# Column-tile projections that share passes with value matmuls, in an attention and MLP kernel on one core

## The chip, the core and the metric

The kernel runs on one core of a Trainium2 chip. The core has a matrix engine (TensorE, PE in the profile), a vector engine (VectorE, DVE), an engine for activation functions (ScalarE, ACT), a general engine (GpSimd, POOL), and SyncE (SP), whose queue issues most of the transfers. The engines run side by side, each with its own instructions in a fixed order, and wait for one another by semaphores. PSUM, the memory that PE writes, has eight banks of 512 fp32 columns here. The metric is the device time of one execution in microseconds (us); less is better.

## The reference

The input is one sequence of 2048 tokens with 512 features. Two blocks read it, and a gate mixes them. `norm` is a layer norm without learned factors, and `shift` moves each quarter of the features by +1, -1, +2 or -2 tokens.

```python
x = A_x                                            # 1 x 2048 x 512
g = sigmoid((x * gate_w).sum(-1))
q, k, v = split(x @ wqkv)                          # 32 heads of 16 features
a = softmax(q @ k.T * 16 ** -0.5) @ v @ wo         # per head, heads side by side
h = gelu(norm(x) @ w1)                             # 512 -> 512
x1 = x + shift(h) @ w2
b = x1 + gelu(norm(x1) @ w3) @ w4                  # 512 -> 1792 -> 512
out = g * a + (1 - g) * b
```

## The kernel before

Attention is most of the work. The queries are taken in four chunks `c` of 512. For each chunk there are 4 groups `G` of 8 heads, and for each group 2 parities `p`: 32 rounds, each of 4 heads at once. A head of a round has 16 key tiles of 128 keys, so a round has 64 score tiles (128 keys by 512 queries) and the kernel 2,048.

A score tile is one matmul with 32 contracted rows (`qk_op`, line 842). Four of them fit beside each other in the array, as row tiles; this mode is called "row". Its exponential is made in one of two ways:

- On ACT (`issue_act`, line 910): two score tiles lie in one PSUM slot of 1024 columns (`psA`, two such slots), and one ACTIVATE (line 922) makes bf16 probabilities of both in a slot of `PA` (8 slots of 1024 columns). Each tile then takes one value matmul. The slot is free again when both have been done.
- On DVE (`issue_dve`, line 932): the tile lies in a `ring` slot of 512 columns (three such slots). DVE turns scores into the bits of a bf16 exponential (line 948). Three shifted copies of a pair of tiles follow, on DVE (line 984) or POOL (line 986), and the sum of four value matmuls smooths the error. So such a tile takes four value matmuls.

A value matmul (`take_pv`, line 1017) contracts 128 keys and writes 17 rows of the accumulator `acc`: the head's sum of probabilities and its 16 features. Each of the four heads of the round has its own column tile of the array, at columns 0, 32, 64 and 96; this mode is called "col". Each column tile has a queue of its own, `pvq[i]`.

Everything else that PE multiplies is a projection: q, k, v, w1 to w4 and the output projection. `gen` (line 525) describes one as a list of units; a unit is four matmuls, one to each column tile (line 532), and all the units add up in one ring slot, which DVE then reads out (`evac`). So scores for DVE and projections share the three ring slots. In this text a pass is a group of up to four matmuls, one to each tile of the array, that run at the same time.

The order of all this is not written by hand. A planner (`Sim`, line 90) plays the engines in the kernel's own build: jobs with a hold time, dependencies, buffers and priorities. `pe_run` (line 190) places matmuls on PE, with a cost `SWITCH` for a change between the row and column modes. What comes out is an order of instructions for each engine, and that order is what the chip runs; no time of the planner's is in it. Whenever the planner's PE is free, `pe_pick` (line 1174) chooses what comes next:

- Score tiles first, if a `psA` slot is free: two for ACT (up to twice), and in the same pass up to `DVE_WAIT` for DVE if a ring slot is free.
- Otherwise column work for at most `MAXU` passes, up to the time at which ACT is expected to give back its slot. `do_gen` takes whole units of the current projection (`cur_gen`, `run_gen` at line 1150): there is one at a time. `do_pv` takes value matmuls, one from each queue that has one ready, for as many passes as keep the filled share over a limit (`PV_FULL`, `PV_IDLE`).
- Otherwise `filler` (line 1258) may put in matmuls with zeros.

`BASE` (line 296) holds the settings of these choices, and `STAGES` (line 321) replaces some of them for each stretch of 32 score tiles (`SEG`). After each round `finish_round` reads `acc` out, and a chain of transfers through SP's queue divides by the sums. At the end of the kernel (lines 1289 to 1344) the last output tiles use the three ring slots and half of a `psA` slot as banks.

Of the kernel before, what the change touches and what calls it, by code (L numbers as in the profile page):

```python
# [47 lines left out]

class Call:
# [28 lines left out]
class Gen:  # L78


    def __init__(self, units, deps, at, name, acq="ring", due=None):
        self.units, self.deps, self.at, self.name = units, deps, at, name
        self.due = due
        self.pos = 0
        self.buf = Buf(acq, 1)
        self.ops = [o for u in units for o in u]
        self.gone = False


class Sim:  # L90
    SWITCH = 95.0
# [64 lines left out]
    def try_engine(self, e):  # L156
        if self.t_free[e] > self.t:
            return False
        best = None
        for j in self.jobs[e]:  # L160
            if j.at > self.tiles:
                continue
            if j.ready is None:
                if any(d.done is None for d in j.deps):
                    continue
                j.ready = self.t
            if any(not self.free[b.cls] for b in j.acq) or j.port and self.lock > self.t:
                continue
            key = (j.prio, j.ready, j.seq)
            if best is None or key < best[0]:  # L170
                best = (key, j)
        if best is None:
            return False
        j = best[1]
        self.jobs[e].remove(j)
        for b in j.acq:
            self.take(b)
        j.start = self.t
        self.emit(self.t, self.in_port_order(e, j.fn) if j.port else j.fn)
        self.t_free[e] = self.t + j.hold  # L180
        if j.port:
            self.lock = self.t + j.hold
        self.busy[e] += j.hold
        self.log.append((e, self.t, j.hold, j.name))
        self.push(self.t + j.hold, None)
        self.pending -= 1
        self.push(self.t + j.hold + j.lat, lambda: self.finish_job(j))
        return True

    def pe_run(self, ops):  # L190
        cur = self.t
        for o in ops:
            if o.mode != self.mode:
                s = max(max(self.arr), cur) + self.SWITCH
                self.mode = o.mode
            elif o.tile is None:
                s = max(max(self.arr), cur)
            else:
                s = max(self.arr[o.tile], cur + self.ISSUE)
# [46 lines left out]
def kernel(  # L246
# [50 lines left out]
        P1_PRIO=0.414,  # L297
        S_PRIO=0.38,
        GP2=0.0,
        GP3=1.0,  # L300
        DVE_STOP=6,
        DVE_STOP_L=8,
        URG=5,
        URG_L=17,
        DVE_ALONE=2,
        EARLY=68,
        SL=(45, 60),
        IDLE_NS=537,
        PD_LOW=0,
# [3 lines left out]
        AHEAD2=9,  # L313
        PV_FULL=0.916,
        PV_IDLE=0.37,
        PRESS=27,
        MAXU=9,
        ROT=0, DUE_SH=0, AT_SH=0,
    )
    SEG = 32  # L320
    STAGES = {0: {'DVE_ALONE': 150, 'EARLY': 2}, 1: {'GP3': 0.6}, 2: {'P1_PRIO': 0.438, 'AT_SH': 120, 'PD_LOW': 2, 'URG_L': 20}, 3: {'DUE_SH': 20, 'URG_L': 19, 'PRESS': 8}, 4: {'GP2': 0.35, 'DVE_WAIT': 4, 'SL': (165, 60), 'URG_L': 14}, 5: {'DVE_STOP_L': 7, 'ROT': 3}, 6: {'ROT': 3, 'URG_L': 20, 'EARLY': 110, 'AT_SH': 120}, 7: {'DVE_STOP': 8}, 8: {'ROT': 2}, 9: {'ROT': 2, 'GP2': 0.2}, 12: {'DVE_STOP_L': 6, 'PA_LOW': 2, 'PV_FULL': 0.686, 'AHEAD2': 10}, 13: {'ROT': 3}, 14: {'GP3': 0.9, 'AT_SH': 120, 'AHEAD2': 10}, 16: {'ROT': 2}, 17: {'URG_L': 16, 'DVE_STOP_L': 6, 'AT_SH': 10, 'PV_IDLE': 0.593}, 18: {'ROT': 2, 'PA_LOW': 3}, 20: {'MAXU': 7, 'AT_SH': 120, 'GP2': 0.35}, 22: {'PV_FULL': 0.805, 'GP2': 0.35}, 23: {'GP2': 0.35}, 25: {'S_PRIO': 0.215, 'DVE_STOP': 7, 'URG': 7}, 26: {'PV_FULL': 0.638, 'DVE_STOP': 8}, 27: {'URG_L': 14, 'PV_IDLE': 0.319, 'DVE_ALONE': 500, 'PD_LOW': 3}, 28: {'DVE_STOP_L': 5, 'PV_FULL': 0.681, 'GP3': 0.8}, 29: {'DVE_WAIT': 4, 'DVE_ALONE': 300, 'URG': 7, 'PV_IDLE': 0.328}, 30: {'PA_LOW': 1, 'URG_L': 19}, 31: {'PA_LOW': 0, 'SL': (165, 180), 'PRESS': 28, 'PD_LOW': 3}, 32: {'DVE_STOP_L': 10, 'P1_PRIO': 0.596, 'ROT': 2, 'S_PRIO': 0.516}, 33: {'PRESS': 54, 'ROT': 3, 'AHEAD2': 7, 'S_PRIO': 0.436}, 34: {'AT_SH': 120, 'P1_PRIO': 0.562, 'AHEAD2': 7}, 35: {'GP3': 0.6}, 36: {'URG': 8, 'AHEAD2': 12}, 37: {'S_PRIO': 0.236, 'AHEAD': 8, 'P1_PRIO': 0.491}, 38: {'P1_PRIO': 0.476, 'ROT': 3}, 39: {'GP3': 0.9, 'AHEAD2': 10, 'URG': 6, 'GP2': 0.1}, 40: {'URG': 3, 'PV_FULL': 0.947, 'DVE_ALONE': 300, 'PD_LOW': 2}, 41: {'DVE_ALONE': 0, 'PV_IDLE': 0.272, 'ROT': 2, 'PD_LOW': 1}, 42: {'DVE_STOP': 7, 'DVE_STOP_L': 10, 'DUE_SH': -8, 'PRESS': 10}, 43: {'URG': 8}, 44: {'GP2': 0.1}, 45: {'URG_L': 18, 'GP2': 0.2}, 46: {'GP3': 0.8}, 47: {'DVE_STOP': 5, 'P1_PRIO': 0.442, 'MAXU': 3, 'PRESS': 11}, 48: {'SL': (5, 20)}, 49: {'SL': (5, 20)}, 50: {'DVE_STOP_L': 5, 'AHEAD2': 8, 'P1_PRIO': 0.218, 'AT_SH': 30}, 51: {'DVE_STOP': 9, 'P1_PRIO': 0.226, 'GP3': 0.6}, 52: {'DVE_WAIT': 5, 'PD_LOW': 3, 'ROT': 2, 'IDLE_NS': 697}, 53: {'ROT': 1}, 54: {'ROT': 1, 'P1_PRIO': 0.201}, 55: {'PA_LOW': 2}, 56: {'EARLY': 60, 'PV_FULL': 0.817, 'P1_PRIO': 0.354}, 57: {'DVE_ALONE': 2, 'PD_LOW': 3}, 58: {'DVE_ALONE': 300, 'GP2': 0.35, 'PRESS': 15}, 59: {'PRESS': 19}, 60: {'DUE_SH': 40, 'PRESS': 20}, 61: {'IDLE_NS': 380}, 62: {'AHEAD': 8, 'GP2': 0.35}, 63: {'ROT': 2}}
# [3 lines left out]
    WIDTHS, RING = (2, 2), 3  # L325

# [9 lines left out]
    def slots(name, n, shape, dt=BF16, where=const):  # L336
# [38 lines left out]
    sim_ring = slots("ring", RING, [P, 512], F32, ps)  # L375
    sim = Sim({
        **{f"psA{w}{n}": slots(f"psA{n}", 1, [P, 512 * w], F32, ps) for n, w in enumerate(WIDTHS)},
        "ring": sim_ring,
        "PA": slots("PA", NPA, [P, 512 * max(WIDTHS)]),
# [145 lines left out]
    def gen(name, at, deps, mms, N=512, due=None):  # L525
# [11 lines left out]
        g = Gen(units, deps, at, name, due=due)  # L537
        gens.append(g)
# [10 lines left out]
    def x_transposes(c, half, dep):  # L549
# [6 lines left out]
        g.ops = [o for u in g.units for o in u]  # L556
        g.buf.users = 2
# [70 lines left out]
    def gate(at):  # L628
# [14 lines left out]
        g2.ops = list(g2.units[0])  # L643
        g2.ops[-1].frees.append(zl)
# [11 lines left out]
        gt.ops = gt.units[0]  # L656
        zb = Buf("ot", 1)
# [252 lines left out]
    def issue_act(got, cls):  # L910
        buf = Buf(cls, 1)
        sim.take(buf)
        ops = []
        for h, (r, (kt, i)) in enumerate(got):
            left[r][i].remove(kt)
            ops.append(qk_op(r, kt, i, lambda h=h: buf.slot[:, h * 512:(h + 1) * 512], buf))
        n = 512 * len(got)
        pb = Buf("PA", len(got))

        hold = 0.833 * n + 67.0  # L920
        exps[:] = [j for j in exps if j.done is None]
        job = act(hold, ops, lambda: nc.scalar.activation(out=pb.slot[:, 0:n], in_=buf.slot[:, 0:n], func=ACT.Exp,  # L922
                                                          scale=0.25), acq=[pb], frees=[buf], prio=3)
        exps.append(job)
        for h, (r, (kt, i)) in enumerate(got):
            c, G, p = rounds[r]
            add_pv(r, i, kt, lambda kt=kt, h_=8 * G + 2 * i + p: V0[:, kt, h_, :],
                   lambda h=h: pb.slot[:, h * 512:(h + 1) * 512], [job, j_v[kt, G // 2]], pb)
            pv_left[r] += 1
# [206 lines left out]
    cur_gen = [None]  # L1136

    def gen_ready():
        if cur_gen[0] is not None:
            return cur_gen[0]  # L1140
# [9 lines left out]
    def run_gen(g, nunits, ops):  # L1150
        if cur_gen[0] is None:
            cur_gen[0] = g
            sim.take(g.buf)
            gens.remove(g)
        took = 0
        while g.pos < len(g.units) and took < nunits:
            ops += g.units[g.pos]
            g.pos += 1
            took += 1
        if g.pos == len(g.units):  # L1160
            cur_gen[0] = None
        return took
# [11 lines left out]
    def pe_pick():  # L1174
# [6 lines left out]
        for _ in range(len(WIDTHS)):  # L1181
# [3 lines left out]
            got = act_tiles(w, used if len(used) + w <= 4 else set())  # L1185
            if not got:
                break
            ops += issue_act(got, f"psA{w}{n}")
# [29 lines left out]

        def do_pv(least):
            m = n - (len(ops) + 3) // 4  # L1220
# [6 lines left out]
            for _ in range(best):  # L1227
                for i in range(4):
                    h = pv_ready(i)
                    if h is not None:  # L1230
                        ops.append(take_pv(i, h))

        def do_gen():
            nonlocal g
            left_ = n - (len(ops) + 3) // 4
            while g is not None and left_ > 0:
                left_ -= run_gen(g, left_, ops)
                g = gen_ready() if g.pos == len(g.units) else None
# [6 lines left out]
        else:  # L1245
            do_gen()
            if (len(ops) + 3) // 4 < n:
# [42 lines left out]
    pB = sim.free["psA%d1" % WIDTHS[1]][0]  # L1290
    bank = [sim_ring[0][:], sim_ring[1][:], sim_ring[2][:], pB[:, 512:1024]]
# [82 lines left out]
```

## Time and profile before

| | |
|---|---|
| time, median of 3 runs | 772.25 us (771.98 to 775.94) |
| span of the profiled execution | 813.8 us |
| profiled span to median | 1.054 |
| ACTIVATEs of probabilities (line 922) | 737 of 1024 columns, so 1,474 score tiles on ACT |
| score tiles on DVE (line 948) | 574 |
| value matmuls (line 1017) | 1,474 + 2,296 = 3,770 |
| first and last ACTIVATE of line 922 begin | 10.6 and 802.7 us |

The profile is of one execution, and for this kernel that execution was longer than the runs without one; its rows say how the time is shared out. The page gives no time around the span, so sums are made against the span of 813.8 us and then scaled to the median. Busy time of an engine is the union of its instructions, so 737 instructions of 1,025 ns each cover 703.1 us: consecutive ones overlap. In the groups the last column is the idle time of that engine just before these instructions, and what ended it. Matmuls overlap too, so the distance between two starts says more than a duration.

### The profile page before, as it was taken

How to read it: one execution, taken by the hardware profiler on the slowest of the kernel's cores; microseconds unless marked ns; L12 is line 12 of the kernel's file. 1: busy time of each engine (PE TensorE's matmuls, PEld its weight loads, DVE VectorE, ACT ScalarE, POOL GpSimd, SP SyncE). 2: the span in 40 equal slices, each digit the busy share in tenths (PEclk: the TensorE clock that was granted, in tenths of full speed). 3: DMA queues.
4: the chain of work that ended last, by engine and by line, in shares of the span. 5: the costliest groups of instructions: out<-in, count | busy, mean ns of one | idle time of the engine just before them, and what ended most of it. 6: DMA issues, size and time to landing. Idle time of an engine off the chain costs nothing.

```text
span 813.8 us, 23989 instructions
## 1 busy us (share of the span) xinstructions
PE 805.9 (99%) x9711; PEld 226.8 (28%) x9711; DVE 739.2 (91%) x1590; ACT 753.2 (93%) x762; POOL 339.7 (42%) x338
## 2 busy tenths in 40 slices
PE   9999999999999999999999999999999999999997
PEld 4333322222322222233222223222222322223222
DVE  6999999999999999999899998888999899998885
ACT  5899999999999999999898999999999998999994
POOL 2243435433544445342443343444543334445442
PEclk9888888888888888888888888888888888888888
DMA  9303210342000140133001001001100000000000
GB/s 203 113 3 58 63 45 18 76 123 75 18 5 19 46 92 18 48 98 92 23 9 34 21 26 37 24 24 45 27 12 19 19 23 19 26 18 19 16 19 31
DMA packets 67094, 34.61 MB, mean 43 GB/s; under 512 B 46748, under 2 KB 62380, under 8 KB 66984
## 3 DMA queue, kind: packets, MB, share of 16 engines
q1 hardware_dynamic: 66040, 32.56, 16.0%
q8 instruction: 76, 1.25, 0.7%
q10 hardware_dynamic: 944, 0.52, 0.2%
q14 instruction: 34, 0.28, 0.1%
HBM read 17.40 MB, written 6.81 MB: 30 GB/s over the span
## 4 chain that ended last, share of the span: by engine, by line
PE 92%; ACT 4%; DVE 2%; DMA 1%; issue 1%; SPq 0%; ACTq 0%; DVEq 0%
PE acc L1017 33%; PE ring L532 28%; PE psA L842 28%; ACT PA L922 2%; PE ring L842 1%; ACT hT L735 1%; ACT hT L766 1%; DVE PD L984 1%; PE acc L1277 0%; PE ring L510 0%; DVE PD L948 0%; DMA pk<-den 0%; ACT L922 0%; DMA xn_dram<-xn 0%; PE ring L1295 0%
## 5 line engine op out<-in xcount | busy, mean ns | idle before, releaser
L922 ACT ACTIVATE PA<-psA 128x1024 bf16<-128x1024 f32 x737 | 703.1, 1025 | 45.0 <-PE acc L1017 12.0
L986 POOL TENSOR_SCALAR PD<-PD 128x1024 uint16<-128x1024 uint16 x276 | 287.3, 1046 | 421.1 <-DVE PD L984 227.8
L948 DVE TENSOR_SCALAR PD<-ring 128x512 uint16<-128x512 f32 x574 | 382.8, 685 | 39.8 <-PE ring L842 30.1
L1017 PE MATMUL acc<-PD,V 128*17 128x512 bf16 x2296 | 319.0, 406 | 0.7 <-DVE PD L984 0.4
L842 PE MATMUL psA<-q,kT 32*128 32x512 bf16 x1474 | 290.3, 394 | 1.9 <-ACT PA L922 1.7
L1017 PE MATMUL acc<-PA,V 128*17 128x512 bf16 x1474 | 288.1, 407 | 0.0
L984 DVE TENSOR_SCALAR PD<-PD 128x1024 uint16<-128x1024 uint16 x585 | 225.4, 426 | 4.5 <-PE acc L1017 2.6
L842 PE MATMUL ring<-q,kT 32*128 32x512 bf16 x574 | 194.6, 395 | 0.0
L842 PEld LDWEIGHTS <-kT 32*128 32x128 bf16 x2048 | 72.2, 91 | 345.0 <-issue 343.8
L1017 PEld LDWEIGHTS <-V 128*17 128x17 bf16 x3770 | 74.7, 90 | 129.4 <-issue 107.6
L532 PE MATMUL ring<-xnT,w 128*32 128x512 bf16 x1152 | 97.4, 412 | 0.0
L532 PE MATMUL ring<-w,hT 128*32 128x512 bf16 x704 | 61.2, 410 | 0.0
L532 PEld LDWEIGHTS <-w 128*32 128x32 bf16 x1920 | 41.3, 97 | 48.0 <-issue 34.6
L1050 POOL TENSOR_TENSOR oT<-accsb,bcs 128x512 bf16<-128x512 f32 x31 | 39.4, 1271 | 25.8 <-DVE PD L984 16.8
L532 PE MATMUL ring<-w,w 128*32 128x256 bf16 (+1 forms) x768 | 42.7, 331 | 0.0
L532 PE MATMUL ring<-w,hB 128*32 128x512 bf16 x448 | 37.9, 412 | 0.0
L1033 DVE COPY accsb<-acc 128x512 f32<-128x512 f32 x31 | 21.3, 687 | 4.6 <-PE acc L1017 4.1
L532 PE MATMUL ring<-w,wq 128*32 128x512 bf16 x256 | 22.9, 415 | 0.0
L765 DVE CAST hT<-ring 128x512 bf16<-128x512 f32 x28 | 19.2, 686 | 3.0 <-PE ring L532 2.9
L675 DVE BATCH_NORM_STATS2 st<-x_sb 128x6 f32<-128x512 bf16 x32 | 21.8, 683 | 0.0
L532 PEld LDWEIGHTS <-hT 128*32 128x32 bf16 x704 | 14.9, 96 | 20.6 <-issue 16.1
L765 DVE CAST hB<-ring 128x512 bf16<-128x512 f32 x28 | 18.9, 679 | 1.9 <-PE ring L532 1.9
(93 smaller groups left out, 288.0 us busy)
## 6 DMA issues: line engine op xcount, KB each, us to landing
bcs<-rr SPq DMA_DIRECT2D x124, 64.0 KB
xn_dram<-xn SPq DMA_DIRECT2D x32, 128.0 KB
w<-in_B_w_dram SPq DMA_DIRECT2D x5, 512.0 KB
oD<-oT SPq DMA_DIRECT2D x124, 16.0 KB
w<-in_B_w_dram SPq DMA_DIRECT2D x4, 448.0 KB
out_dram<-ot SPq DMA_DIRECT2D x14, 128.0 KB
x_sb<-in_A_x_dram SPq DMA_DIRECT2D x3, 512.0 KB
w<-in_A_wqkv_dram SPq DMA_DIRECT2D x2, 256.0 KB
```

What stands on the lines that cost most here:

```text
L532: units.append([Op("col", j, lambda j=j, lf=lf, rf=rf, n0=n0, n1=n1, st=st, sp=sp: nc.tensor.matmul(get()[32 * j:32 * j + 32, n0:n1], lhsT ...
L675: a = dve(600, deps, lambda: nc.vector.bn_stats(out=sb.slot[:], in_=x_sb[:, t, :]), prio=6, at=at, acq=[sb])
L735: ge = act(93 + 1700 * KT + 2600, pre, lambda: nc.scalar.activation(out=hT[:, :, 2:2 + S], in_=hT[:, :, 2:2 + S], func=ACT.Gelu_apprx_tanh ...
L765: pre.append(evac(g, PSUM_NS, lambda ps, m=m: nc.vector.tensor_copy(out=h2()[:, m, :], in_=ps[:])))
L842: o = Op("row", i, lambda: nc.tensor.matmul(dst(), lhsT=kT[G][32 * i:32 * i + 32, kt * P:(kt + 1) * P], rhs=qbuf[G, c].slot[32 * i:32 * i ...
L922: job = act(hold, ops, lambda: nc.scalar.activation(out=pb.slot[:, 0:n], in_=buf.slot[:, 0:n], func=ACT.Exp, scale=0.25), acq=[pb], frees= ...
L948: nc.vector.tensor_scalar(out=pr["buf"].slot[:, h * 512:(h + 1) * 512], in0=buf.slot[:], scalar1=BITS_MUL, scalar2=BITS_ADD, op0=ALU.mult, ...
L984: return nc.vector.tensor_scalar(out=d[k][:, 0:w], in0=d[0][:, 0:w], scalar1=float(SHIFT * k), scalar2=None, op0=ALU.add)
L986: return nc.gpsimd.tensor_scalar(out=d[k][:, 0:w], in0=d[0 if both else 2][:, 0:w], scalar1=1.0, scalar2=float(SHIFT * (k if both else 1)) ...
L1017: o = Op("col", i, lambda: nc.tensor.matmul(acc[32 * i:32 * i + DH + 1, :], lhsT=lhs(), rhs=rhs(), start=st, stop=True, tile_position=(0, ...
L1033: e = dve(PSUM_NS, round_ops[r], lambda: nc.vector.tensor_copy(out=ab.slot[:], in_=acc[:]), acq=[ab], prio=0)
L1050: n = gp(1250, d3, lambda: nc.gpsimd.tensor_tensor(out=ob.slot[:], in0=ab.slot[:], in1=bb.slot[:], op=ALU.mult), acq=[ob], frees=[ab, bb], ...
```

## The change

There are four parts.

**Projections by column tile.** A projection that is marked `skew` no longer moves by whole units. It has a position for each column tile (`cp`), and `take(j)` gives the next matmul of column tile `j`. All projections made by `gen` are marked; the transposes and the two small full-array steps of the gate are not. What a unit frees is freed when all four of its matmuls have been taken.

**Shared passes.** `one_pass` fills a pass column tile by column tile. In a projection pass, a column tile for which the projection has nothing left may take a value matmul (`HOLE` bit 1). In a value pass, a column tile without a ready value matmul may take one of an open projection (bit 2), or open a new one for it (bit 4). Up to `MAXG` projections may be open at once, each with its own ring slot. The budget in passes is now counted (`used`), before it was the number of matmuls over four.

**Single slots.** `PA` is one tile with 16 slots of 512 columns. An ACTIVATE takes a `Run`: slots `a`, `a + d`, ... with any step `d` of 1 to 5, and writes them with a strided access. Each slot is freed by its own value matmul. The seven PSUM banks beside `acc` become one tile `banks`: banks 1 and 2 and banks 4 and 5 are the two slots of ACT, and banks 0, 3 and 6 are the ring. An ACTIVATE of three tiles, with a ring bank beside a pair, is in the code where `TRI` ring slots are free.

**Settings.** `SWITCH` has a value for each mode, new settings (`HOLE`, `MAXG`, `TRI`, `TRIG`) are added, and `BASE` and all of `STAGES` have other values. HOLE is 7 in `BASE`, 2 in stages 3 to 12, and 0 in stages 13 to 20; MAXG is 1 but for stages 8, 9 and 62; TRI is 4 throughout.

```diff
+class Run:
+    def __init__(self, cls, n):
+        self.cls, self.parts = cls, [Buf(cls, 1) for _ in range(n)]
+
+    def find(self, free):
...
+        for d in (1, 2, 3, 4, 5):
+            for a in free:
+                if all(a + d * k in have for k in range(n)):
+                    return a, d
...
@@ class Gen
-        self.gone = False
+        self.cp = [0] * 4
+        self.skew = False
+
+    def take(self, j):
+        k = self.cp[j]
+        if k == len(self.units):
+            return None
+        self.cp[j] = k + 1
+        o = self.units[k][j]
+        if min(self.cp) == k + 1:
+            for x in self.units[k]:
+                if x is not o:
+                    o.frees += x.frees
+                    x.frees = []
+        return o
...
 class Sim:
-    SWITCH = 95.0
+    SWITCH = {"row": 122.0, "col": 96.0, "full": 96.0}
...
     BASE = dict(
-        P1_PRIO=0.414,
+        P1_PRIO=0.686,
...
-        DVE_STOP_L=8,
+        DVE_STOP_L=14,
...
-        PV_IDLE=0.37,
-        PRESS=27,
+        PV_IDLE=0.731,
+        PRESS=18,
         MAXU=9,
-        ROT=0, DUE_SH=0, AT_SH=0,
+        ROT=2, DUE_SH=-14, AT_SH=0, HOLE=7, MAXG=1, TRI=4, TRIG=1,
     )
...
+    PAIRS, SPARE = ((1, 2), (4, 5)), (0, 3, 6)
...
-    sim_ring = slots("ring", RING, [P, 512], F32, ps)
+    banks = ps.tile([P, 7, 512], F32, name="banks")
+    PA = const.tile([P, 2 * NPA, 512], BF16, name="PA")
+    sim_ring = [Bank(banks, i) for i in SPARE]
...
-        pb = Buf("PA", len(got))
+        run = Run("PA", n)
...
+        job = act(hold, ops, lambda: nc.scalar.activation(
+            out=PA[:, run.a:run.a + run.d * (n - 1) + 1:run.d, :], in_=banks[:, at[0]:at[0] + n, :], func=ACT.Exp,
+            scale=0.25), acq=[run], frees=frees, prio=3)
...
+    def gen_op(j, more):
+        for g in active:
+            if g.skew:
+                o = g.take(j)
+                if o is not None:
+                    if not g.left():
+                        active.remove(g)
+                    return o
+        if more and len(active) < K.MAXG and (not active or active[-1].skew):
+            g = gen_new()
+            if g is not None and g.skew:
+                begin(g)
+                return g.take(j)
+        return None
...
+            third = None
+            if len(sim.free["ring"]) >= K.TRI and not used and (K.TRIG or gen_new() is None):
...
+        def one_pass(gen_first):
+            got = []
+            for i in range(4):
+                o = gen_op(i, True) if gen_first else None
+                if o is None:
+                    h = pv_ready(i)
+                    if h is not None and (not gen_first or K.HOLE & 1):
+                        o = take_pv(i, h)
+                    elif not gen_first and K.HOLE & 2:
+                        o = gen_op(i, K.HOLE & 4)
+                if o is not None:
+                    got.append(o)
+            ops.extend(got)
+            used[0] += 1
+            return got
...
             for _ in range(best):
-                for i in range(4):
-                    h = pv_ready(i)
-                    if h is not None:
-                        ops.append(take_pv(i, h))
+                one_pass(False)
```

## The prediction

> **What bounds the kernel now.** I read the page's first and fourth parts first, to see which engine is full and which one the end hangs on.
>
> ```profile
> span 813.8 us, 23989 instructions
> ...
> PE 805.9 (99%) x9711; PEld 226.8 (28%) x9711; DVE 739.2 (91%) x1590; ACT 753.2 (93%) x762; POOL 339.7 (42%) x338
> ...
> PE 92%; ACT 4%; DVE 2%; DMA 1%; issue 1%; SPq 0%; ACTq 0%; DVEq 0%
> ```
>
> Three engines are nearly full, and 92% of the chain that ends last is PE. A busy PE need not be a fast PE, so the next view is busy time by stretch, which shows whether that average hides stages. The columns are window, its length, then PE, PEld, DVE, ACT and POOL busy.
>
> ```profile
> 500.00:600.00 100.00, 100.00 (x1182) 25.37 (x1175) 89.92 (x190) 94.68 (x100) 43.73 (x42) 0.85 0.11 27
> 600.00:700.00 100.00, 100.00 (x1219) 26.71 (x1216) 89.75 (x185) 93.52 (x92) 40.08 (x38) 0.85 0.07 19
> 700.00:800.00 100.00, 99.75 (x1200) 27.11 (x1201) 88.35 (x180) 93.48 (x93) 49.14 (x47) 0.85 0.07 18
> ```
>
> It hides none: PE has no gap, while ACT idles 5 to 6% and DVE 10 to 12%. Next the groups by line, for the price of each piece.
>
> ```profile
> L922 ACT ACTIVATE PA<-psA 128x1024 bf16<-128x1024 f32 x737 | 703.1, 1025 | 45.0 <-PE acc L1017 12.0 <-PE psA L842 11.4 <-PE ring L842 6.6
> L948 DVE TENSOR_SCALAR PD<-ring 128x512 uint16<-128x512 f32 x574 | 382.8, 685 | 39.8 <-PE ring L842 30.1 <-PE psA L842 2.8 <-PE acc L1017 1.6
> L1017 PE MATMUL acc<-PD,V 128*17 128x512 bf16 x2296 | 319.0, 406 | 0.7 <-DVE PD L984 0.4 <-DVE accsb L1033 0.2
> ...
> L1017 PE MATMUL acc<-PA,V 128*17 128x512 bf16 x1474 | 288.1, 407 | 0.0
> ```
>
> ACT and DVE wait for PE; PE waits for nobody (0.7 us before 3,770 value matmuls). So PE's own sequence sets the end. Last the timeline of one stretch of it (start, duration, line, shape, count).
>
> ```profile
> 408.54 0.42 PE L842 MATMUL psA<-q,kT 32*128 32x512 bf16 x2
> 408.54 0.42 PE L842 MATMUL ring<-q,kT 32*128 32x512 bf16 x1
> 408.89 0.38 PE L1017 MATMUL acc<-PD,V 128*17 128x512 bf16 x1
> 408.89 0.38 PE L1017 MATMUL acc<-PA,V 128*17 128x512 bf16 x1
> 408.90 0.38 PE L1017 MATMUL acc<-PD,V 128*17 128x512 bf16 x1
> 409.11 0.41 PE L1017 MATMUL acc<-PA,V 128*17 128x512 bf16 x3
> 409.46 0.39 PE L842 MATMUL psA<-q,kT 32*128 32x512 bf16 x2
> ```
>
> This is one beat of the kernel: a row-tiled score pass, then column-tiled passes, then the next score pass. Up to four matmuls start together, one to each tile: a pass. The two column passes, at 408.89 and 409.11, have three each: in both a column tile is empty, a hole, and they cost as much as full ones.
>
> Now every matmul row of the trace, put into passes by start (within 45 ns). From one start to the next: column to column 230 ns in the mean, score to column 332, column to score 363. There are 737 beats. A beat with one column pass costs 332 + 363 = 695 ns, each further column pass 230. The mean beat is 813.8 / 737 = 1,104 ns, while one ACTIVATE takes ACT 703.1 / 737 = 954 ns. That is why ACT waits.
>
> **The change, part by part.** (1) *Projections by column tile, and shared passes.* Nothing is removed: the 3,770 value matmuls and the projections stay. What can fall is the number of passes. The trace has 1,839 column passes of 512 columns. Their 6,810 matmuls (3,770 values, 3,040 projections) would fill 1,702.5. So at most 136 passes can go: 136 x 0.23 = 31 us. Some of these are one pass split by a wait. Counted safely, within runs of column passes that hold value matmuls alone, there are 336 holes, or 84 passes: 84 x 0.23 = 19.3 us. Those are what an open projection can fill. It needs an operation left for that very column and its operands ready, and in stages 13 to 20 of 65 the setting HOLE is 0. I take 0.65 of it: 55 passes, **-12.6 us**. From below, packing better only inside each run saves 1,839 - 1,792 = 47 passes, 10.8 us. A filled hole costs nothing: value passes of two, three and four matmuls are followed by the next column pass after 223, 223 and 222 ns in the median.
>
> The gain counts in full only while ACT can follow. A beat becomes 12.6 / 737 = 17 ns shorter, 1,087 against ACT's 954, so ACT is not the bound in the mean. The cover that would be needed is there: 45.0 us of idle before L922, some 25 of it outside the first 40 us.
>
> (2) *Single slots for probabilities.* The same memory (8 slots of 1024 columns become 16 of 512), each half free when its own value matmul is done. It removes at most ACT's waits for value matmuls, 12.0 us before L922. These lie beside PE, which is busy then, so they give 0 on the path. If the cover went (ACT the bound), they would give up to 12. A write to two slots that are not neighbours is not in the trace for this line. The nearest row is GELU at L735, which writes four separated runs: 7,031 ns for 8,192 columns, 0.858 ns each, against 6,178 for 7,168 in one run at L766, 0.862. Bounds +/- 1% of 703 us, 7 us of ACT; I take 0, since the nearest row shows no price, and ACT has slack.
>
> (3) *The triple ACTIVATE* needs four free ring slots (TRI=4), and the ring has three. It never fires: 0. The merging of the PSUM tiles keeps the same banks: 0.
>
> (4) *Settings.* These move tiles between ACT and DVE. A tile on DVE costs PE four value matmuls, 230 ns; on ACT it costs a quarter pass and half a beat's score part, 58 + (695 - 230) / 2 = 290. So each tile moved to DVE saves PE 60 ns and costs DVE 382.8 / 574 + 225.4 / 574 = 1.06 us. DVE's idle time of 75 us bounds that at 70 tiles, 4 us of PE either way; I take 0, since some stages raise and others lower the stops that govern it. The 208 filler matmuls (L1277, 17.8 us) show where PE had nothing; they may shrink, and are in no term. No DMA is added, and SP's and POOL's queues keep their jobs, though in another order: 0, with a few us either way, as SP's tasks lie 16% of the time on the DMA engines.
>
> Sum: 813.8 - 12.6 = 801 us of the profiled span. The profiled execution is 5.4% longer than the median of the runs shown, and I scale: 772.25 x (1 - 12.6 / 813.8) = 760, and round up to **761**.
>
> **What is queued behind a wait.** In a shared pass a projection matmul stands behind a value matmul that waits for ACT or DVE. Behind both stand the next score pass, and with it ACT and DVE. Before, 818 passes were pure projections with four matmuls, which wait for a semaphore of nobody but their inputs. The trace so far has little of this: all starts of PE that came later than the usual distance add up to 5.5 us.
>
> The Trainium skill speaks against the change here (TensorE: Matmul & The Clock Gate, Part 3, What overlaps and what doesn't): matmuls start and end strictly in program order, only weight loads are pulled ahead. The trace agrees so far as it shows starts in order only. By that rule a late value matmul stops a projection that could have run, which is the fourth case below.
>
> **The rivals.** *A, as summed* (0.48): 761, its own range 751 to 768. *B, more of it* (0.15): all holes filled, 31 us, so 772.25 x (1 - 31 / 813.8) = 743, with part of it lost to ACT about 748. For it: DVE and ACT idle 5 to 12% in the steady stretches. Against it: ACT's own busy time, 753 us, plus 10.6 before its first exponential and 10 after its last, is 774 of 813.8, so every engine would have to run at 98%. *C, no change* (0.12): passes fall, but ACT and DVE, over 90% busy in each stretch, take the bound, PE idles or fills, and the span stays: 772. For it: the three loads lie within 8%. Against it: 25 us and more of ACT idle time that is PE's doing.
>
> *D, slower* (0.25): waits in shared passes. Its place is the value matmul at the head of a shared pass. With 150 shared passes and 0.18 us of wait each (a fifth of an ACTIVATE's 0.954) it costs 27 us. Less the gain, that is +14 us: 772.25 x (1 + 14 / 813.8) = 786. It decides from 12.6 / 150 = 0.08 us a pass. For it: a probability is often taken soon after its exponential, and the planner's times are not the chip's. Against it: value passes waited for the same results before, for 5.5 us in all. A page's rule for it is named above; its price here comes from the rows.
>
> **How the numbers follow.** A change under 0.5% (768.4 to 776.1) can't be told from none. Faster: A but for a small part, and B: 0.61. Same: C and the edges of A and D: 0.14. Slower: D: 0.25. The range of 8 in 10 runs from B's full packing, 744, to D, 786.
>
> **What would show it.** Right: fewer column passes (about 1,785 for 1,839); in the timeline, starts of L532's successor and L1017's within one pass; ACT's idle time before L922 smaller by about 12 us; no new row of PE waiting for ACT PA or DVE PD. Wrong: passes as many as before; or fewer passes with wider distances, and PE waiting in front of value matmuls (D); or PE below 97% with fillers risen (C). A count of exponentials far from 737 would make the settings, not the sharing, the cause.

## The result, and the profile after

The changed kernel takes 2,431.52 us (median of 4 runs, 2,429.64 to 2,436.29) against 772.12 us before: 3.148 times the time, 95% interval 3.140 to 3.155. The forecast was 761, with a range of 744 to 786. The page of the changed kernel, first and fourth parts:

```profile
span 2427.8 us, 23885 instructions
...
PE 1428.7 (59%) x9602; PEld 327.7 (13%) x9602; DVE 760.1 (31%) x1533; ACT 814.5 (34%) x771; POOL 352.0 (14%) x350
...
PEclk6555555555555555555555555555555555555555
...
PE 43%; ACT 32%; DVE 20%; issue 4%; DVEq 0%; DMA 0%; ACTq 0%
ACT PA L1060 31%; PE banks L658 21%; PE banks L972 18%; DVE PD L1087 15%; PE acc L1156 3%; DVE hB L895 1%; DVE hT L895 1%; DVE hT L863 0%; DVE V L746 0%; DVE x_sb L874 0%; DVE kT L706 0%; DVE qf L729 0%; DVE ot L931 0%; DVE PD L1123 0%; DVEq L1087 0%
```

ACT and DVE work only a little longer (814.5 us for 753.2, 760.1 for 739.2; ACT's exponentials no longer overlap one another), but each now fills a third of the span where it filled over 90%. And the chain that ends last no longer runs along one engine: it holds PE, ACT and DVE, and the four largest lines of it all write or read `banks` (L1060 and L1087 read it, as the groups below show). The same chain in order of time (start, duration, what) for one beat:

```profile
1001.09 1.03 ACT PA L1060
1002.12 0.04 issue
1002.16 0.62 PE banks L972 x2
1002.79 0.03 issue
1002.81 0.02 DVEq L1087
1002.83 0.05 issue
1002.88 0.70 DVE PD L1087
1003.58 0.02 issue
1003.61 1.03 ACT PA L1060
```

ACT reads one bank pair, then PE writes, then DVE reads a ring bank, then ACT again, each beginning within 0.1 us of the end of the one before. No two engines use `banks` at the same time, although they use different banks of it; in this stretch only work that doesn't touch it, like the value matmuls into `acc`, runs beside them. The groups show the same as idle time:

```profile
L1060 ACT ACTIVATE PA<-banks 128x1024 bf16<-128x1024 f32 x746 | 763.9, 1024 | 1543.8 <-PE banks L658 765.4
L1087 DVE TENSOR_SCALAR PD<-banks 128x512 uint16<-128x512 f32 x556 | 384.0, 692 | 1336.3 <-ACT PA L1060 523.4
L972 PE MATMUL banks<-q,kT 32*128 32x512 bf16 x2048 | 460.4, 594 | 502.0 <-DVE PD L1087 241.4
```

DVE's first step waits 523.4 us for ACT, whose data it doesn't read. What the two have in common is the tile `banks`. The page's clock row adds a second cost: the clock granted to PE is 0.518 of full speed in the mean (0.50 to 0.55 in four stages of 100 us), so a score pass is followed by the column pass after 540 ns in the median, for 322 before.

### The profile page after: what moved, and what is told of

It reads as the page before. It is cut to its first block, busy times and chain, and to the rows that moved or that the text cites. A ratio compares the mean times of both kernels' runs of the same rounds, so it can differ in the third digit from the quotient of the medians.

```text
span 2427.8 us, 23885 instructions
## 1 busy us (share of the span) xinstructions
PE 1428.7 (59%) x9602; PEld 327.7 (13%) x9602; DVE 760.1 (31%) x1533; ACT 814.5 (34%) x771; POOL 352.0 (14%) x350
## 4 chain that ended last, share of the span: by engine, by line
PE 43%; ACT 32%; DVE 20%; issue 4%; DVEq 0%; DMA 0%; ACTq 0%
ACT PA L1060 31%; PE banks L658 21%; PE banks L972 18%; DVE PD L1087 15%; PE acc L1156 3%; DVE hB L895 1%; DVE hT L895 1%; DVE hT L863 0%; DVE V L746 0%; DVE x_sb L874 0%; DVE kT L706 0%; DVE qf L729 0%; DVE ot L931 0%; DVE PD L1123 0%; DVEq L1087 0%
## 5 line engine op out<-in xcount | busy, mean ns | idle before, releaser
L1060 ACT ACTIVATE PA<-banks 128x1024 bf16<-128x1024 f32 x746 | 763.9, 1024 | 1543.8 <-PE banks L658 765.4
L1087 DVE TENSOR_SCALAR PD<-banks 128x512 uint16<-128x512 f32 x556 | 384.0, 692 | 1336.3 <-ACT PA L1060 523.4
L972 PE MATMUL banks<-q,kT 32*128 32x512 bf16 x2048 | 460.4, 594 | 502.0 <-DVE PD L1087 241.4
L1125 POOL TENSOR_SCALAR PD<-PD 128x1024 uint16<-128x1024 uint16 x288 | 299.6, 1044 | 1855.6 <-DVE PD L1123 1181.0
L1156 PE MATMUL acc<-PD,V 128*17 128x512 bf16 x2224 | 506.2, 607 | 0.9 <-DVE accsb L1172 0.8
L1156 PE MATMUL acc<-PA,V 128*17 128x512 bf16 x1492 | 465.0, 613 | 0.0
L658 PE MATMUL banks<-xnT,w 128*32 128x512 bf16 x1152 | 177.8, 585 | 142.8 <-ACT PA L1060 89.6
L658 PE MATMUL banks<-w,hT 128*32 128x512 bf16 x704 | 126.0, 597 | 110.4 <-ACT PA L1060 73.7
L658 PE MATMUL banks<-w,hB 128*32 128x512 bf16 x448 | 84.7, 607 | 76.8 <-ACT PA L1060 46.1
L658 PE MATMUL banks<-w,w 128*32 128x256 bf16 (+1 forms) x768 | 79.2, 465 | 73.0 <-ACT PA L1060 48.8
L658 PE MATMUL banks<-wo,oD 128*32 128x512 bf16 x224 | 67.2, 608 | 44.1 <-ACT PA L1060 30.0
L1172 DVE COPY accsb<-acc 128x512 f32<-128x512 f32 x31 | 21.2, 685 | 19.4 <-PE acc L1156 13.5
```

Source lines behind the costliest of these rows:

```text
L658: units.append([Op("col", j, lambda j=j, lf=lf, rf=rf, n0=n0, n1=n1, st=st, sp=sp: nc.tensor.matmul(get()[32 * j:32 * j + 32, n0:n1], lhsT ...
L972: o = Op("row", i, lambda: nc.tensor.matmul(dst(), lhsT=kT[G][32 * i:32 * i + 32, kt * P:(kt + 1) * P], rhs=qbuf[G, c].slot[32 * i:32 * i ...
L1060: job = act(hold, ops, lambda: nc.scalar.activation(out=PA[:, run.a:run.a + run.d * (n - 1) + 1:run.d, :], in_=banks[:, at[0]:at[0] + n, : ...
L1087: nc.vector.tensor_scalar(out=pr["buf"].slot[:, h * 512:(h + 1) * 512], in0=buf.slot[:], scalar1=BITS_MUL, scalar2=BITS_ADD, op0=ALU.mult, ...
L1125: return nc.gpsimd.tensor_scalar(out=d[k][:, 0:w], in0=d[0 if both else 2][:, 0:w], scalar1=1.0, scalar2=float(SHIFT * (k if both else 1)) ...
L1156: o = Op("col", i, lambda: nc.tensor.matmul(acc[32 * i:32 * i + DH + 1, :], lhsT=lhs(), rhs=rhs(), start=st, stop=True, tile_position=(0, ...
```

## The experiments

Two questions were open: what made the factor of three, and what the change is worth without it. Every ratio is to the kernel before in the same job.

**e1: the PSUM in five tiles again.** All else is as in the changed kernel.

```diff
-    banks = ps.tile([P, 7, 512], F32, name="banks")
+    pair_of = {a: ps.tile([P, 2, 512], F32, name=f"pair{a}") for a, _ in PAIRS}
+    ring_of = {i: ps.tile([P, 1, 512], F32, name=f"ring{i}") for i in SPARE}
...
-    sim_ring = [Bank(banks, i) for i in SPARE]
+    sim_ring = [Bank(ring_of[i], 0) for i in SPARE]
...
```

> The changed kernel with its PSUM in five tiles again (two pairs of two banks, three single banks); sharing, single slots and all settings stay. Theory S (the one tile for seven banks makes every user of any bank wait for the user before it): 750 to 790 us, PE over 95% busy, and no row in which PE waits for ACT PA for more than 10 us. Rival P (the one tile of probability slots with strided writes is what serialises): stays over 1500 us. Rival W (PE waits in shared passes, case D of the prediction, or the settings): 800 to 2400 us with PE waiting in front of value matmuls.

Measured: 773.85 us, ratio 1.0018 (1.0000 to 1.0036). Its page, its group of exponentials and DVE's first step:

```profile
span 771.4 us, 23591 instructions
...
PE 753.4 (98%) x9602; PEld 223.4 (29%) x9602; DVE 718.3 (93%) x1533; ACT 742.7 (96%) x771; POOL 352.8 (46%) x350
...
L1061 ACT ACTIVATE PA<-pair 128x1024 bf16<-128x1024 f32 x746 | 692.6, 1075 | 15.0 <-PE ring L973 6.3
L1088 DVE TENSOR_SCALAR PD<-ring 128x512 uint16<-128x512 f32 x556 | 366.8, 680 | 29.1 <-PE ring L973 26.6
```

DVE's first step no longer waits for ACT. So the one PSUM tile costs 2,431.52 - 773.85 = 1,658 us, and what is left of the change can't be told from nothing: the interval touches 1. Rivals P and W fall: probability slots, shared passes and settings are all in this kernel.

**e2: the kernel before, with its seven banks in one tile.** The converse. The order isn't touched.

```diff
-    sim_ring = slots("ring", RING, [P, 512], F32, ps)
+    banks = ps.tile([P, 7, 512], F32, name="banks")
+    sim_ring = [banks[:, i, :] for i in (0, 3, 6)]
+    two = [banks[:, i:i + 2, :].rearrange("p a b -> p (a b)") for i in (1, 4)]
...
```

> The kernel before, its order unchanged, with its seven PSUM banks as parts of one tile. Theory S: 2000 us or more, with the three-step beat PE, DVE, ACT one after the other and the PE clock near 0.52. Rivals P and W: 772 us, since neither the probability slots nor the order changed.

Measured: 2,365.41 us, ratio 3.064 (3.053 to 3.076), clock 0.525. Of its waits (who waits for whom, us, times, longest):

```profile
DVE PD L950 <- ACT PA L924: 526.6, 219, 6.3
...
PE banks L844 <- DVE PD L950: 282.4, 239, 2.1
```

The same cross waits as after the change, in the order of before. One tile for seven banks is enough.

**e3: the kernel before, with its probability slots in one SBUF tile.**

```diff
+    pa_all = const.tile([P, NPA, 512 * max(WIDTHS)], BF16, name="PA")
...
-        "PA": slots("PA", NPA, [P, 512 * max(WIDTHS)]),
+        "PA": [pa_all[:, i, :] for i in range(NPA)],
```

> The kernel before, with its eight probability slots as parts of one SBUF tile (whole slots, no strided write). Theory S says that only PSUM banks in one tile serialise: 772 us within 0.5%. Rival P: over 1000 us, ACT waiting for value matmuls.

Measured: 771.2 us, ratio 0.9999 (0.9979 to 1.0019). Parts of one SBUF tile don't exclude each other. This run is of use for a second reason: it is the order of before, profiled at a granted clock of 0.999. The profiled execution of before, which the prediction read, had 0.851.

```profile
span 769.5 us, 23989 instructions
...
PE 756.1 (98%) x9711; PEld 224.8 (29%) x9711; DVE 730.8 (95%) x1590; ACT 735.9 (96%) x762; POOL 339.7 (44%) x338
...
PE 69%; ACT 19%; DVE 8%; issue 3%; DMA 1%; SPq 1%; POOL 0%; DVEq 0%; POOLq 0%; ACTq 0%
...
L923 ACT ACTIVATE PA<-psA 128x1024 bf16<-128x1024 f32 x737 | 686.0, 1052 | 19.1 <-PE psA L843 9.3
```

Its stages (window, length, then PE, PEld, DVE, ACT, POOL busy, the granted clock and the transfers):

```profile
500.00:600.00 100.00, 99.95 (x1273) 27.05 (x1269) 96.18 (x205) 99.07 (x105) 47.04 (x45) 1.00 0.12 26
600.00:700.00 100.00, 100.00 (x1300) 27.67 (x1289) 95.56 (x198) 97.60 (x101) 45.47 (x43) 1.00 0.09 24
```

At the full clock there is little slack: ACT is busy 98 to 99% in these stages, not 94, and idles 19.1 us before its exponentials, not 45.0. The chain that ends last holds 69% of PE and 19% of ACT, not 92 and 4.

**e4 and e5: only the ring, only the pairs.** The kernel before with its three ring banks in one tile, and with its two pairs in one tile.

```diff
+    rings = ps.tile([P, RING, 512], F32, name="rings")            # e4
+    sim_ring = [rings[:, i, :] for i in range(RING)]
...
+    pairs = ps.tile([P, 4, 512], F32, name="pairs")               # e5
+    two = [pairs[:, i:i + 2, :].rearrange("p a b -> p (a b)") for i in (0, 2)]
...
```

> The kernel before, its order unchanged, with only the three ring banks in one tile; the two pairs stay tiles of their own. Theory T (a PSUM tile has one user at a time, whatever bank of it is used): DVE's reads of the ring, some 510 us, and PE's writes of it, some 350 us, exclude each other, while ACT's pairs are free of them: 900 to 1400 us, PE waiting for DVE PD and not for ACT PA. Rival B (the seven-bank size of the tile, or a tile shared with ACT, is what serialises): 772 us.

> The kernel before, its order unchanged, with only the two pairs in one tile. Theory T: the second pair no longer covers the first, a beat is one ACTIVATE and one score pass, 1.03 + 0.33 us and two hand-overs of 0.05: 737 x 1.45 = 1070 us, 950 to 1200, PE waiting for ACT PA alone. Rival B: 772 us.

Measured: 1,130.9 us (ratio 1.464, 1.455 to 1.473; clock 0.925) and 1,280.16 us (1.657, 1.646 to 1.669; clock 0.823). Two waits of e4, and one of e5:

```profile
PE rings L533 <- DVE PD L949: 124.8, 198, 1.1
...
PE rings L843 <- DVE PD L949: 32.0, 80, 0.9
```

```profile
PE pairs L844 <- ACT PA L924: 301.4, 596, 1.5
```

Theory T holds: the exclusion goes by tile, not by size, and reaches just the engines that use that tile. With the ring in one tile PE waits for DVE (and 0.6 us for ACT before its pairs), with the pairs in one tile for ACT. The time of e4 lies in its range of 900 to 1,400. The size for e5 was too low by 210 us, outside its 950 to 1,200. The chain that ended last shows what it left out:

```profile
ACT PA L924 51%; PE pairs L844 26%; PE acc L1019 7%; PE ring L534 6%; PE ring L844 2%; ACT L924 0%; ACTq L924 0%; ACT L768 0%; PE ring L512 0%; PE ring L1297 0%; ACT w L563 0%; ACT L737 0%; PE ring L642 0%; PE pairs L1297 0%; DVE q L595 0%
```

Score passes for ACT hold about 450 ns of it a beat (26% of 1,283.6 us, over 737 beats), where 330 were counted. Another 13% is value and projection matmuls of PE, which the forecast had left off the chain.

**e6: split tiles, new settings, no sharing.** HOLE is 0 everywhere and `g.skew = True` is left out.

> The changed kernel with split PSUM tiles, its new settings and single slots, but projections by whole units and no shared passes. Theory P (PE's passes set the time, so what sharing saved is worth it): some 48 passes more than with sharing, 48 x 0.22 = 10 us, about 784 us. Theory A (at the full clock ACT is the bound, and passes lie beside it): the time goes with the number of ACTIVATEs; within 1% of the split kernel's 773.9 if that number is near 746.

**e7: split tiles, sharing, old settings.** BASE, STAGES and SWITCH are those of before, with HOLE 7.

> The changed kernel with split PSUM tiles, shared passes and single slots, but BASE, STAGES and SWITCH of the kernel before (HOLE 7). Theory P: fewer passes than the 1832 of before, and faster than 772 us by 0.22 us for each. Theory A: 772 us plus or minus 1.0 us for each ACTIVATE more or fewer than 737. Rival O (an order needs settings chosen for it): over 780 us, with idle time before ACT's and DVE's instructions.

Measured: 805.89 us (1.0434, 1.0393 to 1.0475) and 801.04 us (1.0371, 1.0325 to 1.0418). Both theories on the size of sharing fail: ACT has 742 and 740 ACTIVATEs, fewer than the 746 of e1, and waits 40.2 and 46.9 us before them. Taking sharing away and adding it both cost some 4%. That pointed to rival O: the settings belong to one exact order.

**e8, e9, e10: one nanosecond.** The planner's constant `PE_LAT`, 275 ns, is moved by 1 in the kernel before (276), in e1 (274) and in e6 (274). Nothing else changes, but the planner's first choice that falls otherwise makes all later ones new, so each is an order for which nobody chose the settings.

> The kernel before with one constant of its planner changed by a nanosecond (PE_LAT 276 for 275); no setting and no mechanism is touched. Theory F (the settings are fitted to one exact order; any other order is an unfitted one, and that costs 3 to 4%, as in the two runs with sharing removed or settings exchanged): 790 to 810 us, with ACT idle time before its exponentials near 40 us. Rival M (the time comes from the mechanisms and the settings' sense): 772 us within 0.5%.

> The changed kernel with split PSUM tiles and PE_LAT 274 for 275. Theory F: 780 to 800 us where the fitted order had 773.9. Set against the run without sharing (805.9, same settings, an unfitted order too) it gives what sharing is worth with fitting out of the way: by theory G (sharing saves passes and time) 790 or less; by rival N (sharing gives nothing) 800 to 812.

> The changed kernel with split PSUM tiles, without sharing, and PE_LAT 274: a second unfitted order, to see how far such orders scatter. Theory F with G: 800 to 812, close to 805.9 and over the shared one by 10 us or more. Rival N: within 5 us of the shared one.

Measured: e8 790.76 us (1.0237, 1.0192 to 1.0283), e9 795.81 (1.0294, 1.0239 to 1.0348), e10 801.40 (1.0387, 1.0309 to 1.0465). Theory F holds: a nanosecond costs the kernel before 2.4%, e1 2.8% (795.81 / 773.85). In e8's group the loss shows as idle time of ACT, 41.7 us for 19.1 in e3:

```profile
L922 ACT ACTIVATE PA<-psA 128x1024 bf16<-128x1024 f32 x735 | 684.5, 1057 | 41.7 <-PE acc L1017 19.2 <-PE psA L842 17.7 <-PE ring L842 3.0
```

On sharing, e9 against e6 and e10 (795.8 against 805.9 and 801.4) lies between what theories G and N expected: it is inside the scatter of unfitted orders. With the old settings the sign is even the other way: e7, which shares passes, took 801.0 us, e8, which doesn't, 790.8. To settle it, both sides must be fitted alike.

**e11 and e12: both fitted alike.** For e1's kernel, and for e6's without sharing, all 65 stages of STAGES were chosen anew by the same search with the same effort.

```diff
     STAGES = {
-        0: {'URG': 2, 'AHEAD': 24, 'SL': (200, 200), 'PRESS': 24},
+        0: {'URG': 2, 'AHEAD': 24, 'SL': (200, 200), 'PRESS': 24, 'MAXU': 3, 'MAXG': 1},
...
```

> The changed kernel with split PSUM tiles, sharing and single slots, and STAGES fitted anew for exactly this order (the same search for this kernel and for the next, which differ in sharing alone). Theory G (sharing is worth about 1% once both orders are fitted): under 770 us and 5 to 12 us below the next kernel, with fewer column passes and less ACT idle time before its exponentials (under 20 us). Rival N (sharing is worth nothing; only fitting is): within 3 us of the next kernel.

> The same without sharing, its STAGES fitted by the same search for as long. Theory F: far below the unfitted 801 to 806 us of the same mechanism. Theory G: 772 to 780 us, and 5 to 12 us above the kernel with sharing. Rival N: 764 to 771.

Measured: with sharing 770.76 us (0.9992, 0.9982 to 1.0001), without 779.29 (1.0094, 1.0079 to 1.0108). The groups of exponentials, with and without:

```profile
L1061 ACT ACTIVATE PA<-pair 128x1024 bf16<-128x1024 f32 x742 | 687.7, 1086 | 14.6 <-PE pair L973 5.3 <-PE acc L1157 5.0 <-PE ring L973 2.8
```

```profile
L1060 ACT ACTIVATE PA<-pair 128x1024 bf16<-128x1024 f32 x741 | 686.0, 1092 | 23.7 <-PE pair L972 9.2 <-PE ring L972 6.8 <-PE acc L1156 6.8
```

The two differ by 8.5 us or 1.1%: 1,790 column passes of 512 columns for 1,812, and 9.1 us less ACT idle time, at nearly the same number of exponentials (742 and 741). Theory G's difference is met (5 to 12), its "under 770" is missed by 0.8.

That sharing is worth this much isn't shown, for each side is one fit. The runs tell how far fits differ: e1 and e11 are one kernel with two sets of STAGES, and lie 3.1 us apart. The kernel before shares nothing either, by e8 its settings are fitted to its order too, and it takes 771.76 us, 7.5 less than e12 (which also has the single slots and the new BASE and SWITCH). Nor do passes order the times: 1,832 take 771.2 us (e3), 1,812 take 779.3 (e12), 1,790 take 770.8 (e11), 1,784 take 773.9 (e1). The kernel before and e11 can't be told apart, and no version run here is measurably faster than the kernel before.

## Why the prediction was wrong, point by point

**The step that failed** is the last sentence of part (3): "The merging of the PSUM tiles keeps the same banks: 0." It measured +1,658 us in the changed kernel (after against e1) and +1,594 in the old order (e2). The banks are the same, but the program's waits go by tile: users of one PSUM tile were kept apart whichever bank they use. These are semaphore waits that the program's instructions carry. Of the 3,552 projection matmuls, whose ring banks ACT's exponentials never use, 272 wait for a semaphore that ACT counts up after the change, and 3 in e1. DVE's first step has 439 such waits for 1, and ACT's exponentials have 522 waits for DVE's semaphore for none. The Trainium skill (PSUM — Partial Sum Buffer, PSUM bank collisions raise a hardware error) says that the hardware neither arbitrates nor stalls, and that engines on different banks run clean. In e3 and e1 the trace agrees: PE, ACT and DVE were 93% and more busy side by side in seven banks. So it isn't the chip that asks for these waits.

How the price comes about: ACT's 763.9 us, DVE's 384.0 and PE's writes lie one behind another. In the chain, ACT PA has 31.2% of 2,428 us, 757 us, which is nearly all of ACT's exponentials; DVE PD has 15.4%, 374 of 384; PE banks 39.1%, 949. The rest are the read-outs, value matmuls and the hand-overs. PE's part is longer for the low clock: a score matmul lasts 594 ns, for 384 in e1. How much of the 949 us that is wasn't tried.

**Case D** was nearest in sign and wrong in mechanism. No wait in a shared pass is needed: e1 has all the shared passes, and PE idles 2.1 us before its value matmuls there (L1157), 3.6 in e3. The Trainium skill's rule of strict order (TensorE: Matmul & The Clock Gate, Part 3, What overlaps and what doesn't) is that matmuls start and end in program order. No run here speaks against it, and its price was small: the waits of PE that the profile names add up to 8.3 us in e3 and 12.6 in e1, and 3.9 of the 12.6 are a projection's wait for a transfer.

**Part (1), shared passes.** The mechanism works: projection and value matmuls start within 45 ns of each other in 173 passes of e1, and in 54 of e3, which shares nothing and has them as close neighbours alone. The number of column passes was met, 1,784 in e1 where I expected about 1,785, for 1,832 in e3, but partly by luck: 18 tiles went from DVE to ACT (556 on DVE for 574), which takes away 54 value matmuls, or 13.5 full passes. So some 35 passes are left for sharing, and I had taken 55. The time was wrong, for two reasons, whose shares no run separates. First, the sum was made on an execution at 0.851 of the clock. There PE was alone the bound; at the full clock a beat is 769.5 / 737 = 1,044 ns against ACT's 686.0 / 737 = 931, and ACT fills 98 to 99% of the two steady stages above. I had noted the 5.4% between profile and median and scaled by it, but the page's clock line said why, and the scaling kept shares that hold at the low clock alone. Second, PE's saving was given back within PE: by the starts of all its passes, column to column fell by 10.7 us (281.1 to 270.4), while score to column rose by 1.9, column to score by 8.7 (238.1 to 246.8) and score to score by 2.0. The sum is +1.9 us, just the difference of the spans (771.4 and 769.5). There are 746 ACTIVATEs for 737, and ten more changes of mode each way.

With both sides fitted (e11, e12) the difference is -8.5 us, where part (1) said -12.6 on the slow profile, -12.0 on the median. The 22 passes between them are worth 22 x 0.2215 = 4.9 us of it at the full clock; whether the rest is sharing's or the fit's stays open.

**Part (2), single slots: 0.** Not tried alone. ACT's waits for value matmuls fell from 6.4 us (e3) to 3.8 (e1), of which sharing and settings have a part; an ACTIVATE's share of ACT's busy time is 692.6 / 746 = 928 ns against 931, and where no two overlap one lasts 1,024 ns after the change and 1,023 in e2, so the strided write shows no price. The SBUF tile in itself costs nothing (e3).

**Part (4), settings: 0, +/- 4 us.** Mis-sized the most after the tile, as the experiments show it; in the change itself the settings can't be told from the rest. I priced them as tiles moved between ACT and DVE. They are a fit to one order, and the orders off that fit lie 19 to 34 us over the kernel before (e6 to e10). This is why "settings chosen anew" can't be taken as a term of its own.

**The triple ACTIVATE** never fires: all 746 ACTIVATEs of the probabilities have 1,024 columns.

**Case C** (passes fall and the span stays) is what the change does once the tile is split: 1.0018. Its mechanism is met in part only: PE stays 98% busy and the fillers fall from 208 to 153, where C had it idle or fill.

## What to carry to other kernels

Before costing a merged buffer at nothing, ask what unit the waits go by: here parts of one SBUF tile were independent, parts of one PSUM tile were not, and that was worth a factor of three. In the profile after, look whether several engines share the chain and all its large pieces use one tile; and before trusting a profile's shares, compare its granted clock with that of other executions. Where an order comes from a planner, a mechanism can be judged only with both sides fitted alike, and more than once: a 1 ns change in the planner moved the time by more than twice the 8.5 us between the two fits.

## What the runs showed of the hardware

The granted clock fell with PE's share of busy time: 0.999 with PE 98% busy (e3), 0.925 with 81% (e4), 0.823 with 76% (e5), 0.525 and 0.518 with 59% (e2 and after the change). In these five traces its records hold two values alone, 1.0 and 0.5: after the change PE had half the clock for 2,344 of 2,428 us, in e4 for 171 of 1,126. The idle pieces needn't be long for that: the longest gap of PE's after the change is 2.6 us. So a wait in front of PE cost twice here, once by itself and once in slower matmuls: column passes 401 ns apart in the median, for 221 in e1.

One execution of a dense kernel on this single core ran at 0.850 from 7 us to its end (the profile of before: 813.8 us, against 769.5 for the same order at 0.999 in e3), with no difference in the program that would explain it; its cause stays open.

A change between row and column mode costs about 105 ns each way at the full clock (e3: 325 and 327 ns from start to start in the mean, against 221.5 between column passes), and a column pass with holes lasts as long as a full one (e3: 221 ns to the next column pass in the median, for value passes of two, three and four matmuls).
